# A planned attention-and-MLP kernel on one core: the second softmax's scores read in a burst, plans a batch deeper, batch 0's rows transposed on TensorE, output evictions chosen by stretch

## The chip, the core and the metric

The kernel runs on one core of a Trainium2 chip. A core has TensorE for matrix products (PE in the profile, PEld for its weight loads), VectorE (DVE), ScalarE (ACT), GpSimd (POOL) and SyncE (SP). They run at the same time, each through its own instruction queue in order, and wait for each other through semaphores. SyncE issues all DMA transfers of this kernel, between DRAM and the on-chip memory SBUF. PSUM holds TensorE's results and has eight banks of 128 partitions x 512 fp32. The metric is the device time of one execution in microseconds; lower is better.

## What is computed

```python
def mab(q, kv):                      # attention with kv as keys and values
    s = scale * (q @ kv.transpose(0, 2, 1))
    s = s - s.max(-1, keepdims=True)
    a = np.exp(s)
    a /= a.sum(-1, keepdims=True) + 1e-09
    return a @ kv
h = mab(I, x)                        # x: 4 x 12480 x 128, I: 32 inducing rows for each batch
y = mab(x, h).reshape(-1, 128)       # every row of x attends to the 32 rows of h
r = np.maximum(y @ w_in, 0.0)        # w_in: 128 x 2048
return (r * r) @ w_out               # w_out: 2048 x 128
```

There are two softmaxes. The first is over the 12480 rows of a batch, for each of 32 inducing rows, and gives `h`. The second is over the 32 rows of `h`, for each row of `x`. The MLP with a squared relu follows.

## The kernel before

Each of the four batches has 12480 rows. They are cut into 26 chunks of 480 rows, or into seven groups (six of four chunks, one of two); `WID` is a group's width in one of four quarters, 480 or 240 columns. x comes from DRAM in two layouts: `xT` (channels on partitions; the scores' moving operand, one load of 960 KB to a group into a tile `xp`) and `xn` (rows on partitions; the first softmax's values, in 13 halves of 448 or 512 KB into the five buffers `xnb`).

The kernel does not multiply by `w_in` row by row. Since y is a weighted mean of the 32 rows of h, the MLP's hidden values are linear in the 32 weights, and a batch's MLP is rewritten as a quadratic form of those weights. The work of a batch has four background parts, written as Python generators, and a foreground:

- `first(b)`, line 268: seven score steps (four products into one PSUM bank of the pool `ps_a`, then L298 on DVE, which scales them into `sT` and takes their maximum), then the overall maximum, exponentials on ACT (L323), 32x32 transposes on DVE (L333) and the weighted sum over `xn` on TensorE (`hacc`, L345). Each group's `hacc` is copied or added to `hq` on DVE (L351, L353). At its end stands `hT` (L365). The five first `xnb` loads are issued at score step 3, and each later one when a half has been used (`load_xn`, line 275).
- `prepare(b)`, line 457: products of `hT` with the weights, a long chain of small DVE instructions, products of columns on DVE (`G`, L518), and four weight products on TensorE (`wq`, L527) that give `st.w16`, the stationary operands of the foreground's last product.
- `second(b, G)`, line 368: scores of a group against `hT`, transposed on DVE into a tile `e2` of a pool of two (L381), maximum (L383), subtraction on POOL (L387), exponential on ACT (L388), sums and reciprocal on DVE (L391 to L393), product on POOL (L394), transpose back (L397), rounding to fp16 (L404 on ACT or L406 on DVE, and L407), and a store to a DRAM buffer `ad` (L408).
- `squares(b, G)`, line 433: loads `dT` from `ad` (L428), makes single squares (L442 into a bank of `ps_a`, L448, and L452 on POOL) and puts them into `dT` by DMA (L454).
- The foreground is the chunk. `up` (L638) multiplies `dT` by constant pairs into two double banks `hp`; `lift` (L647, twice to a chunk) squares them on ACT; `down` (L653, L654) multiplies by `w16` and `lin` into `po` (two banks of the pool `ps_o`); an eviction to `o` on ACT (L657) or DVE (L659), and the store (L660). Which engine evicts is decided while the program is written, by `to_act`, which keeps estimated totals for both.

The order: a prologue narrows the 64-bit weights on DVE (`narrow`, lines 236 to 242), runs `first(0)`, `prepare(0)` and the first two groups of `second(0, ...)`. Then 104 chunks run, and between them `background(k)` steps generators from a list `plan` by due times in chunk units. `spread(gen, steps, start, length)` enters `steps` steps from `start` on. `head` is the due time of `prepare(b)`, 26b the batch's first chunk. The program's instructions are then put in order at build time by a simulated timeline (`schedule_with_timeline_sim=True`): an instruction that is not ready there can be passed by later ones, so a due time sets a priority and not a place. SP's DMA issues are one such queue.

An `xp` tile (nine buffers, `NX`) is filled by `load_xT` (line 255), read by `first`'s scores and again by `second`'s; its buffer comes free for the next batch only then. So `second`'s reads, due at `reads[b, G]`, set when the next batch's loads can start.

A branch at the end, not taken here, recomputes everything in another way if a check on the data fails.

Of the kernel before, what the change touches and what calls it, by code (L numbers as in the profile page):

```python
# [17 lines left out]
P = 128  # L18
NB = 4
# [10 lines left out]
NQ = 4  # L30
MX = 16
# [15 lines left out]
def attend_then_relu2_mlp(ctx: ExitStack, tc: tile.TileContext, xn, xT, indT, w_in, w_out, outT):  # L47
# [168 lines left out]
    def load_words(src, name):  # L216
        wd = start.tile([P, 512, 2], U32, tag="words", name=name, bufs=6)
        nc.sync.dma_start(wd.rearrange("p (f d) w -> p f (d w)", d=P) if len(src.shape) == 3 else wd.rearrange("p n w -> p (n w)"), src)
        return wd

    def load_rows(j):
        wd = start.tile([P, 512, 2], U32, tag="words", name=f"wo{j}", bufs=6)
# [31 lines left out]

    def load_xT(b, G, again=False):
# [12 lines left out]
    def first(b):  # L268
# [6 lines left out]
        def load_xn(h):  # L275

            if h >= 2 * NG - 1:
                return None
            t = xnb[h % XB]
            rows = xn[b, 4 * CH * (h // 2):min(4 * CH * (h // 2 + 1), NT)]  # L280
            if h < 2 * NG - 2:
                k = 8 - h % 2
                nc.sync.dma_start(t[:, 0:k], rows.rearrange("(p t) c -> p t c", t=15)[:, 8 * (h % 2):8 * (h % 2) + k])
            else:
                nc.sync.dma_start(t[:, 0:7], rows[0:7 * P].rearrange("(p t) c -> p t c", t=7))
                for q in range(4):
                    nc.sync.dma_start(t[32 * q:32 * q + 16, 7], rows[7 * P + 16 * q:7 * P + 16 * q + 16])
            return t
# [14 lines left out]
        xns = xns or {h: load_xn(h) for h in range(XB)}  # L303
# [25 lines left out]
        hq = work.tile([P, P + 1], F32, tag="hq", name=f"hq_{b}", bufs=1)  # L329
        for G, nb32 in enumerate(BLK):  # L330
# [8 lines left out]
            hacc = side_psum(f"hacc_{b}_{G}")  # L339
            for t in range(nb32):  # L340
                if t % 8 == 0:
                    h = 2 * G + t // 8
                    xg = xns.pop(h)
                q = t % 4
                st.last = nc.tensor.matmul(  # L345
                    hacc[32 * q:32 * q + 32, 0:P], en[:, t], xg[:, t % 8], start=t < 4, stop=t + 4 >= nb32,
                )
                if t % 8 == 7 or t == nb32 - 1:
                    xns[h + XB] = load_xn(h + XB)
            if G == 0:  # L350
                nc.vector.tensor_copy(hq[:, 0:P], hacc[:, 0:P])  # L351
            else:
                nc.vector.tensor_tensor(hq[:, 0:P], hacc[:, 0:P], hq[:, 0:P], op=ALU.add)  # L353
            if G == NG - 1:
# [13 lines left out]
    def second(b, G, again=False):  # L368
# [10 lines left out]
        e = work.tile([P, 15, MI], F32, tag="e2", name=f"e2_{b}_{G}")  # L379
        ef = e.rearrange("p t i -> p (t i)")  # L380
        nc.vector.transpose(ef[:, 0:wb], ps[:, 0:wb])  # L381
        mx = work.tile([P, 15], F32, tag="mx2", name=f"mx2_{b}_{G}")
# [50 lines left out]
    def squares(b, G):  # L433
# [6 lines left out]
        ps = att_psum(f"sq_{b}_{G}")  # L440
# [187 lines left out]
    class Chunk:  # L628
# [14 lines left out]
        def lift(self, j):  # L643
# [3 lines left out]
            nc.scalar.activation(self.g[:, 2 * j:2 * j + 2], self.hp.pop(j)[:, 0:2, 0:CH], AF.Square)  # L647

        def down(self):
# [6 lines left out]
            if to_act(220 + 0.833 * CH, 110 + 1.042 * CH):  # L656
                nc.scalar.activation(o, po[:, 0:CH], AF.Identity, bias=st.bias, scale=st.osc)  # L657
# [16 lines left out]
    for G in range(NG):  # L674
        sts[0].xp[G] = load_xT(0, G)
# [34 lines left out]
    plan = []  # L710
# [9 lines left out]
    reads = {}  # L720
# [22 lines left out]
    spread(smallest(), 1, reads[NB - 1, NG - 1] + 3, 0)  # L743
# [11 lines left out]
    soon = chain(second(0, 0), second(0, 1))  # L755
# [11 lines left out]
    for n, chunk in enumerate(chunks):  # L767
        nxt = chunks[n + 1] if n + 1 < len(chunks) else None
        for j in (0, 1):
            chunk.lift(j)  # L770
            if nxt:
                nxt.up(j)
            if j == 0 and n:
                done = chunks[n - 1].down()
# [6 lines left out]
    chunks[-1].down()  # L781
# [192 lines left out]
```

## Time and profile before

| | us |
|---|---|
| median of 3 runs | 462.41 |
| lowest, highest run | 461.12, 466.04 |
| profiled execution | 464.73 |
| its span in the profile | 463.0 |
| first lift of the loop (start) | 87.10 |
| last lift of the loop (start) | 454.47 |

The profile records one execution. Engine lines give busy time, its share of the span and the number of instructions. Groups are named by source line, engine, operation, output and inputs by the program's names; behind the bar stand total busy time and the mean in ns, then the idle time of the engine just before them and what ended most of it. In a table by stage each row is a stretch of the span in us, its length, and busy us with the number of instructions for each engine, then the granted TensorE clock, the share of the DMA engines and GB/s. Rows of the timeline begin with start and duration in us; a bracket tells how long the engine was idle before and what released it.

### The profile page before, as it was taken

The page shows a single profiled execution, that of the slowest core. Times are in us where ns is not written, and L with a number is a line of the kernel's source. Part 1 is how long each engine was busy: PE and PEld are TensorE (multiplying, and loading weights), DVE is VectorE, ACT ScalarE, POOL GpSimd, SP SyncE. Part 2 cuts the span into 40 slices and gives each one's busy share as a digit, 9 for nine tenths or more (in the row PEclk, how much of TensorE's full clock was granted, in tenths as well). Part 3 has the DMA queues.
Part 4 walks back from the last instruction along what each step waited for, and adds up shares of the span by engine and source line. Part 5 has one row for each costly group of instructions (what it writes and reads, how often), then busy time and mean ns, then how long its engine had stood idle before and what let it go on. Part 6 is the DMA issues. An engine that isn't in the chain of part 4 may idle for free.

```text
span 463.0 us, 8566 instructions
## 1 busy us (share of the span) xinstructions
PE 366.8 (79%) x2979; PEld 163.2 (35%) x2979; DVE 325.7 (70%) x902; ACT 282.0 (61%) x397; POOL 85.9 (19%) x93
## 2 busy tenths in 40 slices
PE   0644744899979889878789888988879898788994
PEld 0003413543335333333244234433433344343441
DVE  8969378685643199497561899689626999996442
ACT  1004123479994497437567798566666878067993
POOL 1000011141210030232200132144100423340000
PEclk9999975699979799799599999999999999999998
DMA  7999980377759983667889958644794354337432
GB/s 296 421 248 392 372 295 24 97 240 249 207 173 337 335 277 101 197 188 187 266 276 293 344 195 244 195 138 145 240 290 154 102 167 165 101 128 231 151 136 105
DMA packets 64771, 100.71 MB, mean 218 GB/s; under 512 B 22992, under 2 KB 53968, under 8 KB 64720
## 3 DMA queue, kind: packets, MB, share of 16 engines
q1 hardware_dynamic: 64720, 100.09, 66.3%
q8 instruction: 25, 0.41, 0.4%
q14 instruction: 26, 0.21, 0.1%
HBM read 64.91 MB, written 31.95 MB: 209 GB/s over the span
## 4 chain that ended last, share of the span: by engine, by line
PE 30%; DVE 28%; DMA 26%; ACT 6%; issue 5%; SPq 2%; POOL 1%; ACTq 0%; DVEq 0%; POOLq 0%
DMA xnb<-xn_dram 8%; PE hp L638 8%; PE po L653 7%; ACT g L647 5%; DMA outT_dram<-o 5%; PE s L264 4%; PE hacc L345 4%; DMA xp_False<-xT_dram 4%; DMA dT<-zz 3%; DVE o L659 3%; DVE G L518 3%; DVE a L407 2%; PE wq L527 2%; DMA wo<-w_out_dram 2%; DMA dT<-ad 2%
## 5 line engine op out<-in xcount | busy, mean ns | idle before, releaser
L647 ACT ACTIVATE g<-hp 128x960 f16<-128x960 f32 x208 | 194.4, 974 | 60.7 <-PE hp L638 48.2
L638 PE MATMUL hp<-dT,pairs 96*128 96x480 f16 x416 | 121.4, 381 | 7.3 <-ACT g L647 4.9
L653 PE MATMUL po<-g,w 128*128 128x480 f16 x416 | 115.8, 377 | 7.6 <-ACT o L657 3.4
L387 POOL TENSOR_TENSOR e<-e,mx 128x480 f32<-128x480 f32 (+1 forms) x28 | 28.0, 999 | 232.2 <-DVE mx L383 76.3
L659 DVE TENSOR_SCALAR o<-po,osc,bias 128x480 f32<-128x480 f32 x60 | 45.4, 763 | 30.5 <-PE po L654 17.8
L653 PEld LDWEIGHTS <-w 128*128 128x128 f16 x416 | 40.6, 100 | 60.7 <-issue 19.3
L638 PEld LDWEIGHTS <-pairs 96*128 96x128 f16 x416 | 35.8, 101 | 66.6 <-issue 42.1
L345 PE MATMUL hacc<-xnb,en 128*32 128x128 f32 x784 | 38.3, 324 | 16.8 <-DMA xnb<-xn_dram 8.7
L264 PE MATMUL s<-xp_False,indT_sb 128*32 128x480 f32 (+1 forms) x224 | 32.9, 665 | 22.4 <-DMA xp_False<-xT_dram 12.1
L654 PE MATMUL po<-dT,lin 128*128 128x480 f16 x104 | 39.1, 379 | 7.7 <-DMA dT<-zz 7.5
L452 POOL TENSOR_TENSOR zz<-z 128x480 f16<-128x480 f32 (+1 forms) x28 | 30.2, 1078 | 66.3 <-DVE z L448 39.8
L323 ACT ACTIVATE sT<-sT,nb 128x480 f32<-128x480 f32 (+1 forms) x28 | 18.2, 658 | 33.5 <-DVE nb L316 33.5
L394 POOL TENSOR_TENSOR e<-e,z 128x480 f32<-128x480 f32 (+1 forms) x28 | 27.0, 967 | 56.1 <-DVE z L393 36.9
L345 PEld LDWEIGHTS hacc<-xnb,en 128*32 128x32 f32 x784 | 24.4, 126 | 33.6 <-DMA xnb<-xn_dram 9.7
L657 ACT ACTIVATE o<-po,bias,osc 128x480 f32<-128x480 f32 x44 | 33.0, 762 | 5.2 <-DMA outT_dram<-o 4.4
L353 DVE TENSOR_TENSOR hq<-hacc,hq 128x128 f32<-128x128 f32 x24 | 7.0, 291 | 37.6 <-PE hacc L345 37.6
L264 PE MATMUL s<-xp_False,hT 128*32 128x480 f32 (+1 forms) x224 | 27.7, 563 | 4.3 <-DVE k L195 1.4
L448 DVE TENSOR_SCALAR z<-sq,off,cut 128x480 f32<-128x480 f32 (+1 forms) x28 | 21.5, 767 | 9.3 <-PE sq L442 9.3
L518 DVE TENSOR_TENSOR G<-hwp,hw 128x512 f16<-128x512 f16 x64 | 24.9, 455 | 4.1 <-PE wq L527 4.1
L388 ACT ACTIVATE e<-e 128x480 f32<-128x480 f32 (+1 forms) x28 | 16.2, 578 | 17.0 <-POOL e L387 17.0
L404 ACT ACTIVATE a<-a,lessen 128x480 f16<-128x480 f32 (+1 forms) x20 | 13.6, 681 | 16.5 <-DVE a L397 16.3
L298 DVE TENSOR_SCALAR_CACHE_REDUCE sT<-s 128x480 f32<-128x480 f32 (+1 forms) x28 | 17.0, 608 | 9.1 <-PE s L264 9.1
(190 smaller groups left out, 419.2 us busy)
## 6 DMA issues: line engine op xcount, KB each, us to landing
outT_dram<-o SPq DMA_DIRECT2D x104, 240.0 KB, 2.8
xp_False<-xT_dram SPq DMA_DIRECT2D x24, 960.0 KB, 6.8
xnb<-xn_dram SPq DMA_DIRECT2D x28, 448.0 KB, 5.2
xnb<-xn_dram SPq DMA_DIRECT2D x24, 512.0 KB, 5.9
dT<-ad SPq DMA_DIRECT2D x72, 120.0 KB, 2.6
ad<-a SPq DMA_DIRECT2D x24, 240.0 KB, 2.5
dT<-zz SPq DMA_DIRECT2D x104, 30.0 KB, 2.3
wi<-w_in_dram SPq DMA_DIRECT2D x4, 512.0 KB, 5.6
```

The lines of the kernel that those rows point to most:

```text
L264: nc.tensor.matmul(ps[32 * q:32 * q + 32, 0:w], lhsT, xp[:, w * q:w * q + w], start=True, stop=True,)
L345: st.last = nc.tensor.matmul(hacc[32 * q:32 * q + 32, 0:P], en[:, t], xg[:, t % 8], start=t < 4, stop=t + 4 >= nb32,)
L387: nc.gpsimd.tensor_tensor(e[:, 0:t], e[:, 0:t], mx[:, 0:t].unsqueeze(2).broadcast_to([P, t, MI]), op=ALU.subtract)
L394: nc.gpsimd.tensor_tensor(e[:, 0:t], e[:, 0:t], z[:, 0:t].unsqueeze(2).broadcast_to([P, t, MI]), op=ALU.mult)
L452: nc.gpsimd.tensor_tensor(g[rows], zv[rows], zv[rows], op=ALU.mult)
L518: tt(g[:, :, MI * j:MI * j + n], hwp[:, :, 0:n], hw16f[:, :, s0:s0 + n], op=ALU.mult)
L638: nc.tensor.matmul(hp[:, i, 0:CH].rearrange("p (q t) -> p q t", q=4), pairs[0:96, (2 * j + i) * P:(2 * j + i + 1) * P], self.dT[0:96], sta ...
L647: nc.scalar.activation(self.g[:, 2 * j:2 * j + 2], self.hp.pop(j)[:, 0:2, 0:CH], AF.Square)
L653: nc.tensor.matmul(po[:, 0:CH], st.w16[:, i], self.g[:, i], start=i == 0, stop=False)
L654: done = [nc.tensor.matmul(po[:, 0:CH].rearrange("p (q t) -> p q t", q=4), st.lin, self.dT, start=False, stop=True)]
L657: nc.scalar.activation(o, po[:, 0:CH], AF.Identity, bias=st.bias, scale=st.osc)
L659: done.append(nc.vector.tensor_scalar(o, po[:, 0:CH], st.osc, st.bias, op0=ALU.mult, op1=ALU.add))
```

## The change

1. `second` keeps its transposed scores in a resident tile `scored` of eight slots and yields right after the transpose, so that a step of its own reads `xp`. In the plan that step is due at `reads[b, G]` (`READ`), and the other four at `rests[b, G]` (`REST`). The next batch's load of the group is due 0.4 chunk units after the read. `NX` is seven for nine. `head` of batch b may be as early as 26(b-1) + 0.6; before it was 26b - 17.
2. Batch 0's `xT` is not loaded. Its 13 halves of `xn` all have places of their own from the start (`homes`: the five `xnb`, four in `scored`, four in tiles that are used later), and `turn` transposes them on TensorE, 15 blocks of 128x128 to a group, into `hp` banks, from where ACT copies them to `xp`.
3. `hacc` is one PSUM bank over all seven groups, copied once; the adds to `hq` go.
4. The eviction of `po` goes to ACT in the stretches from a `head` to 18 chunks after it (`heavy`), and to DVE elsewhere; the last one goes to ACT.
5. The products of `squares` go into the `po` banks in place of `ps_a`'s; the 64-bit weight words have four buffers for six.

```diff
-NX = 9
+NX = 7
+HEAVY = 18
-MOST = 17
-PACE = (1.2, 2, 2, 3)
-EARLY = -1
+SLOTS = 8
+READ = (0, 2, 1, 1)
+REST = 2.6
...
+        def turn(G):
+            w = WID[G]
+            xp = st.xp[G] = flow.tile([P, 4 * CH], F32, tag="xp", name=f"xp_{b}_{G}", bufs=NX)[:, 0:4 * w]
+            to = xp.rearrange("p (q n) -> p q n", q=4)
+            for h in range(2 * G, min(2 * G + 2, HALVES)):
+                k = 8 - h % 2
+                ps = two_banks(f"xt_{h}").rearrange("p a (t c) -> p (a t) c", c=P)
+                for t in range(k):
+                    nc.tensor.transpose(ps[:, t], xns[h][:, t], ident)
+                whole = k if h < HALVES - 1 else 7
+                c0 = 256 * (h % 2)
+                nc.scalar.copy(
+                    to[:, :, c0:c0 + 32 * whole].rearrange("p q (t r) -> p t q r", r=32),
+                    ps[:, 0:whole].rearrange("p t (q r) -> p t q r", q=4),
+                )
...
-        xns = {}
+        xns = st.rows if not b else {}
         for G, w in enumerate(WID):
             if b and G == 3:
                 xns = {h: load_xn(h) for h in range(XB)}
+            if not b:
+                turn(G)
...
-            hacc = side_psum(f"hacc_{b}_{G}")
+            hacc = hacc or side_psum(f"hacc_{b}")
...
-            if G == 0:
+            if G == NG - 1:
                 nc.vector.tensor_copy(hq[:, 0:P], hacc[:, 0:P])
-            else:
-                nc.vector.tensor_tensor(hq[:, 0:P], hacc[:, 0:P], hq[:, 0:P], op=ALU.add)
...
-        e = work.tile([P, 15, MI], F32, tag="e2", name=f"e2_{b}_{G}")
+        if again:
+            e = work.tile([P, 15, MI], F32, tag="e2", name=f"e2_{b}_{G}")
+        else:
+            k = 480 * ((NG * b + G) % SLOTS)
+            e = scored[:, k:k + 480].rearrange("p (t i) -> p t i", i=MI)
         ef = e.rearrange("p t i -> p (t i)")
         nc.vector.transpose(ef[:, 0:wb], ps[:, 0:wb])
+        yield
...
-        ps = att_psum(f"sq_{b}_{G}")
+        ps = ps_o.tile([P, 512], F32, tag="po", name=f"sq_{b}_{G}")
...
-            if to_act(220 + 0.833 * CH, 110 + 1.042 * CH):
+            if act:
...
-    for G in range(NG):
-        sts[0].xp[G] = load_xT(0, G)
+    scored = flow.tile([P, SLOTS * 480], F32, tag="scored", name="scored", bufs=1)
+    homes = list(xnb)
...
+    sts[0].rows = {h: load_half(0, h, homes[h]) for h in range(HALVES)}
...
+    scored_by = {(b, G): second(b, G) for b in range(NB) for G in range(NG)}
     for b in range(NB):
-        head = -3.5
+        head = -4
         if b:
             sums = first(b)
             for G in range(NG):
-                free = max(0, G + NG - NX)
-                start = max(reads[b - 1, free] + 0.6, EARLY if b == 1 else -9)
+                start = reads[b - 1, G] + 0.4
                 spread(loads(b, G), 1, start, 0)
-                spread(sums, 1, start + 3, 0)
-            start += 3.5
+                start = max(start + 2.5, 26 * (b - 2) + 7 + 1.4 * G)
+                spread(sums, 1, start, 0)
+            start += 1
             spread(sums, 18, start, LONG)
-            head = max(start + LONG + LAG, 26 * b - MOST)
+            head = max(start + LONG + LAG, 26 * (b - 1) + 0.6)
             spread(prepare(b), 19, head, WEIGHTS)
+        busy.append((head, head + HEAVY))
         for G in range(NG):
-            reads[b, G] = head + 0.5 + PACE[b] * G
+            gen = scored_by[b, G]
+            reads[b, G] = head + 0.5 + (READ[b] if b else 0.4) * G
+            rest = rests[b, G] = max(reads[b, G] + 0.6, head + 1 + REST * G if b else 4 * G - 10)
             if b or G > 1:
-                spread(second(b, G), 4, reads[b, G], 2)
+                spread(gen, 1, reads[b, G], 0)
+                spread(gen, 4, rest, 2)
             if b or G > 0:
-                start = max(26 * b + 4 * G - 9, reads[b, G] + 2.1)
+                start = max(26 * b + 4 * G - 9, rest + 2.1)
...
-                done = chunks[n - 1].down()
+                done += chunks[n - 1].down(heavy(n - 1))
...
-    chunks[-1].down()
+    chunks[-1].down(True)
```

More of the change, by code (lines that the diff above doesn't have):

```diff
@@ L221, in load_rows @@
     def load_rows(j):
-        wd = start.tile([P, 512, 2], U32, tag="words", name=f"wo{j}", bufs=6)
+        wd = start.tile([P, 512, 2], U32, tag="words", name=f"wo{j}", bufs=4)
         for q in range(4):
@@ L252, in prepare_w_out, with load_half @@
         nc.scalar.mul(w_hi, wo_sb, t)
+    def load_half(b, h, t):
+        rows = xn[b, 4 * CH * (h // 2):min(4 * CH * (h // 2 + 1), NT)]
+        if h < HALVES - 1:
+            k = 8 - h % 2
+            nc.sync.dma_start(t[:, 0:k], rows.rearrange("(p t) c -> p t c", t=15)[:, 8 * (h % 2):8 * (h % 2) + k])
+        else:
+            nc.sync.dma_start(t[:, 0:7], rows[0:7 * P].rearrange("(p t) c -> p t c", t=7))
+            for q in range(4):
+                nc.sync.dma_start(t[32 * q:32 * q + 16, 7], rows[7 * P + 16 * q:7 * P + 16 * q + 16])
+        return t
     def load_xT(b, G, again=False):
@@ L275, in load_xn @@
         def load_xn(h):
[L277 to L281, printed above, removed]
-                k = 8 - h % 2
-                nc.sync.dma_start(t[:, 0:k], rows.rearrange("(p t) c -> p t c", t=15)[:, 8 * (h % 2):8 * (h % 2) + k])
-            else:
[L285 to L288, printed above, removed]
-        xns = {}
+            return load_half(b, h, xnb[h % XB]) if h < HALVES else None
+        def turn(G):
[3 more added lines that the diff above has]
+            for h in range(2 * G, min(2 * G + 2, HALVES)):
+                k = 8 - h % 2
+                ps = two_banks(f"xt_{h}").rearrange("p a (t c) -> p (a t) c", c=P)
[7 more added lines that the diff above has]
+                )
+                if whole < k:
+                    nc.scalar.copy(to[:, :, 224:240], ps[:, 7].rearrange("p (q r) -> p q r", q=4)[:, :, 0:16])
+        xns = st.rows if not b else {}
         for G, w in enumerate(WID):
@@ L301, in first @@
             yield
-        xns = xns or {h: load_xn(h) for h in range(XB)}
         m1 = small("m1")
@@ L329, in first @@
         hq = work.tile([P, P + 1], F32, tag="hq", name=f"hq_{b}", bufs=1)
+        hacc = None
         for G, nb32 in enumerate(BLK):
@@ L345, in first @@
                 st.last = nc.tensor.matmul(
-                    hacc[32 * q:32 * q + 32, 0:P], en[:, t], xg[:, t % 8], start=t < 4, stop=t + 4 >= nb32,
+                    hacc[32 * q:32 * q + 32, 0:P], en[:, t], xg[:, t % 8], start=G == 0 and t < 4, stop=G == NG - 1 and t + 4 >= nb32,
                 )
-                if t % 8 == 7 or t == nb32 - 1:
+                if b and (t % 8 == 7 or t == nb32 - 1):
                     xns[h + XB] = load_xn(h + XB)
-            if G == 0:
+            if G == NG - 1:
                 nc.vector.tensor_copy(hq[:, 0:P], hacc[:, 0:P])
-            else:
-                nc.vector.tensor_tensor(hq[:, 0:P], hacc[:, 0:P], hq[:, 0:P], op=ALU.add)
-            if G == NG - 1:
                 nc.vector.tensor_reduce(hq[:, P:P + 1], zs, axis=AX.X, op=ALU.add)
@@ L655, in down @@
             o = work.tile([P, CH], F32, tag="o", name=f"o_{self.b}_{self.c}", bufs=3)
-            if to_act(220 + 0.833 * CH, 110 + 1.042 * CH):
-                nc.scalar.activation(o, po[:, 0:CH], AF.Identity, bias=st.bias, scale=st.osc)
+            if act:
+                done.append(nc.scalar.activation(o, po[:, 0:CH], AF.Identity, bias=st.bias, scale=st.osc))
             else:
@@ L673, in attend_then_relu2_mlp @@
     w_words = [load_words(w_in[:, 1024 * j:1024 * j + 1024], f"wi{j}") for j in range(4)]
-    for G in range(NG):
-        sts[0].xp[G] = load_xT(0, G)
+    scored = flow.tile([P, SLOTS * 480], F32, tag="scored", name="scored", bufs=1)
+    homes = list(xnb)
+    for t0, t1 in ((0, 7), (7, 15), (15, 22), (22, 30)):
+        homes.append(scored[:, t0 * P:t1 * P].rearrange("p (t c) -> p t c", c=P))
+    homes += [flow.tile([P, 8, P], F32, tag="G", name=f"place{i}", bufs=2) for i in range(2)]
+    homes += [start.tile([P, 8, P], F32, tag="rows", name=f"rows{i}", bufs=2) for i in range(2)]
+    nc.vector.memset(homes[HALVES - 1][:, 7], 0.0)
+    sts[0].rows = {h: load_half(0, h, homes[h]) for h in range(HALVES)}
     def weights():
@@ L708, in smallest, with heavy @@
         yield
-    plan = []
+    plan, busy = [], []
+    def heavy(n):
+        return any(a <= n < z for a, z in busy)
     def spread(gen, steps, start, length):
@@ L718, in loads @@
         yield
-    reads = {}
+    reads, rests = {}, {}
+    scored_by = {(b, G): second(b, G) for b in range(NB) for G in range(NG)}
     for b in range(NB):
-        head = -3.5
+        head = -4
         if b:
@@ L753, in background @@
             due = next(todo, None)
-    soon = chain(second(0, 0), second(0, 1))
+    soon = chain(scored_by[0, 0], scored_by[0, 1])
     for n, _ in enumerate(prepare(0)):
@@ L769, in attend_then_relu2_mlp @@
         for j in (0, 1):
-            chunk.lift(j)
+            done = [chunk.lift(j)]
             if nxt:
```

10 lines of the change are left out of this document (6 added, 4 removed).

## The prediction, made before the changed kernel was built or run

> **What bounds the kernel now.** I read the page's busy shares first, then the busy time by stage, then the ACT lifts by stage as the clock of the loop, then the rows at the slow stages.
>
> ```profile
> PE 366.8 (79%) x2979; PEld 163.2 (35%) x2979; DVE 325.7 (70%) x902; ACT 282.0 (61%) x397; POOL 85.9 (19%) x93
> L647 ACT ACTIVATE g<-hp 128x960 f16<-128x960 f32 x208 | 194.4, 974 | 60.7 <-PE hp L638 48.2
> L659 DVE TENSOR_SCALAR o<-po,osc,bias 128x480 f32<-128x480 f32 x60 | 45.4, 763 | 30.5 <-PE po L654 17.8
> L657 ACT ACTIVATE o<-po,bias,osc 128x480 f32<-128x480 f32 x44 | 33.0, 762 | 5.2 <-DMA outT_dram<-o 4.4
> L353 DVE TENSOR_TENSOR hq<-hacc,hq 128x128 f32<-128x128 f32 x24 | 7.0, 291 | 37.6 <-PE hacc L345 37.6
> ```
>
> No engine is full over the span, so the answer lies in stages. Next, busy time by stage (columns: PE, PEld, DVE, ACT, POOL, granted clock, DMA share, GB/s); the last row is the whole loop.
>
> ```profile
> 0.00:60.00 60.00, 27.20 (x263) 10.74 (x267) 44.31 (x133) 7.95 (x17) 1.19 (x9) 1.00 0.98 347
> 60.00:87.00 27.00, 12.77 (x127) 7.68 (x120) 21.64 (x82) 7.47 (x12) 4.12 (x4) 0.58 0.44 145
> 87.00:136.00 49.00, 46.27 (x315) 18.12 (x313) 32.35 (x85) 43.83 (x68) 14.05 (x15) 0.95 0.64 204
> 136.00:163.00 27.00, 23.98 (x263) 12.26 (x263) 7.57 (x21) 15.09 (x20) 0.00 (x0) 0.81 0.92 309
> 256.00:325.00 69.00, 60.15 (x465) 25.60 (x463) 60.11 (x170) 51.89 (x77) 21.37 (x19) 1.00 0.65 205
> 355.00:390.00 35.00, 31.71 (x225) 14.00 (x226) 35.00 (x93) 29.43 (x39) 10.75 (x10) 1.00 0.37 119
> 390.00:410.00 20.00, 15.27 (x142) 7.94 (x141) 18.90 (x53) 5.92 (x9) 7.10 (x8) 0.91 0.41 125
> ...
> 87.00:459.00 372.00, 326.88 (x2595) 144.77 (x2593) 259.78 (x688) 266.56 (x368) 80.59 (x80) 0.95 0.64 204
> ```
>
> Before 60 us the DMA queues are full (0.98). In the loop DVE and ACT have nearly equal work, 259.78 and 266.56 us of 372, but at different times: 87 to 136 is ACT's, 136 to 163 is a transfer's (DVE 7.57 of 27), 355 to 410 is DVE's. The lifts alone (two to a chunk) show what that costs:
>
> ```profile
> 136.00:163.00 27.00, 11.52 (x13) 0.81 0.92 309
> 163.00:195.00 32.00, 14.38 (x16) 0.89 0.62 196
> 195.00:214.00 19.00, 4.02 (x5) 1.00 0.53 157
> 256.00:325.00 69.00, 33.77 (x36) 1.00 0.65 205
> 355.00:390.00 35.00, 25.37 (x28) 1.00 0.37 119
> 390.00:410.00 20.00, 4.29 (x5) 0.91 0.41 125
> 410.00:459.00 49.00, 40.61 (x44) 1.00 0.51 170
> ```
>
> Two stages nearly stop: 195 to 214 and 390 to 410, five lifts each. In both, the last weight product of a batch's `prepare` comes near the end, and only then do `po` and the lifts go on:
>
> ```profile
> 208.98 1.05 PE L527 MATMUL wq<-w_hi,G 128*128 128x128 f16 x16 [1.10 <-DVE wm L529]
> 210.91 0.38 PE L653 MATMUL po<-g,w 128*128 128x480 f16 x1
> ...
> 405.42 1.06 PE L527 MATMUL wq<-w_hi,G 128*128 128x128 f16 x16
> 407.64 0.38 PE L653 MATMUL po<-g,w 128*128 128x480 f16 x1 [0.80 <-DVE w L179]
> ```
>
> So the first chunks of batches 1 and 3 wait for a `prepare` that is late, while DVE (18.90 of 20) does it together with second's softmax and ACT (5.92) starves. After 410 nothing is left for the background and a lift costs 49/44 = 1.11 us.
>
> **The change, part by part.** Terms are against the profiled execution: 464.73 us, of which 463.0 are span; the median of the runs is 462.41, 2.3 below it, and I take that off at the end.
>
> *1. Plan a batch deeper.* By the plan's formulas prepare(b) begins at chunk 13.9, 35.0, 61.0 (b = 1, 2, 3) before, and at 10.8, 35.2, 53.6 after (for b = 3 after: second's last read of batch 2 at 35.2 + 0.5 + 6 = 41.7, its load 0.4 on, the score 2.5 on, then 1 + LONG + LAG = 9). Batch 1 gains 3 chunks, batch 2 nothing, batch 3 over 7. Three chunks at the pace of 256 to 325 (69/36 = 1.92 us a lift, 3.8 a chunk) are 11 us of lead, against a stall of 19 us less the five lifts' own 9.6: the stall of batch 1 goes, 9.4 us. Batch 3 has 28 us of lead against 20 us less 5 x 35/28 = 6.3: 13.7 us go. Bounds: 0 (the lead is eaten on the way) to 23.1; I take 23.1, as each lead is longer than its stall. Next late in their place are `dT` loads.
>
> *2. Second's scores in a burst.* Score matmuls and first transpose of each group are the same instructions, moved forward into eight resident slots; groups of batch 0 are then finished over 4G-10 in place of 1.2G-3 chunks. That moves work from 87 to 136, where ACT is nearly full (43.83 of 49), into 136 to 163. These rows price it and the reads:
>
> ```profile
> L381 DVE STREAM_TRANSPOSE e<-s 128x480 f32<-128x480 f32 x24 | 16.2, 674 | 3.5 <-PE s L264 3.3
> L388 ACT ACTIVATE e<-e 128x480 f32<-128x480 f32 (+1 forms) x28 | 16.2, 578 | 17.0 <-POOL e L387 17.0
> L404 ACT ACTIVATE a<-a,lessen 128x480 f16<-128x480 f32 (+1 forms) x20 | 13.6, 681 | 16.5 <-DVE a L397 16.3
> ```
>
> Five groups x (0.58 + 0.68) = 6.3 us of ACT. Bounds 0 and 6.3; I take 6.3, since the receiving stage has ACT free (15.09 of 27). Five more reads come before the first chunk (5 x 0.67 = 3.4 us); DVE's idle 5.4 us of 60 to 87 cover them, and without that cover they cost the 3.4.
>
> *3. Loads pulled forward.* With the rows of batch 0 read early, seven loads of batch 1 go out at once, ahead of `ad` and `dT` on the one SP queue, and the `xnb` loads right behind them. The last of seven such loads at the start took this long to land:
>
> ```profile
> xp_False<-xT_dram SPq DMA_DIRECT2D x1, 480.0 KB, 17.8
> 81.71 2.59 SPq L428 DMA_DIRECT2D dT<-ad  x5
> ```
>
> A `dT` of the prologue queued behind them waits 0 to 15 us. DMA is busy 0.44 in 60 to 87, so most should have landed; I take +3.
>
> *4. Evictions by stretch.* Heavy stretches hold 65 chunks (18 each, the first 29 joined) and the last goes to ACT too: 66 on ACT for 44, so 22 x 0.76 = 16.6 us leave DVE and 22 x 0.75 = 16.5 join ACT. Where it tells, 355 to 390, DVE is at 35.00 and ACT at 29.43; the stage's evictions on DVE are
>
> ```profile
> 355.00:390.00 35.00, 8.80 (x12) 1.00 0.37 119
> ```
>
> and with them ACT would need 38, more than 35: alone this gains nothing there. Level, both need 32.2. Bounds +3 and -5; I take -3 with the earlier prepare.
>
> *5. hacc kept in PSUM, squares' matmul in `po`'s buffers.* 21 adds of 0.29 us leave the loop's DVE (6.1 us). On the path the hacc stage waits for `xnb`, so 0 (bounds 0 to -6). A `po` buffer held until DVE's `z` can stop `down`: 0 to 0.76 a group, a pass like L659's. Taken as 0 together.
>
> *6. Startup.* 6.4 MB of xT loads go (some 18 us of a full queue at 347 GB/s). New: 98 transposes, 14 PSUM copies on ACT (idle there, 7.95 of 60, 1 us each by the lift). The old rows:
>
> ```profile
> 12.11 1.83 PE L264 MATMUL s<-xp_False,indT_sb 128*32 128x480 f32 x8 [12.11 <-DMA xp_False<-xT_dram]
> 29.94 1.03 PE L264 MATMUL s<-xp_False,indT_sb 128*32 128x240 f32 x8 [1.76 <-DVE sT L298]
> 37.41 1.93 PE L345 MATMUL hacc<-xnb,en 128*32 128x128 f32 x30 [2.11 <-DVE en L333]
> 54.15 2.02 PE L345 MATMUL hacc<-xnb,en 128*32 128x128 f32 x30 [0.40 <-DVE hq L353]
> 59.37 0.19 DVE L365 TENSOR_TENSOR hT<-hs,zr 128x32 f32<-128x32 f32 x1
> 97.77 1.01 PE L264 MATMUL s<-xp_False,hT 128*32 128x480 f32 x8
> 99.53 0.49 PE L617 MATMUL cm<-ident,cm 128*1 128x128 f32 x3
> 211.73 0.27 PE L617 MATMUL cm<-ident,cm 128*1 128x128 f32 x1
> 75.00 0.50 PEld L546 LDWEIGHTS pl<-inc,before 128*128 128x128 f32 x2 [2.53 <-issue]
> ```
>
> A score group takes 1.83 us here and 1.01 later: TensorE runs at half rate (the clock column's 1.00 before its first record says nothing). A transpose follows the last at (0.49 - 0.27)/2 = 0.11 us at full rate, so 0.22 at half; its weight load is 0.25. At half rate: 98 x 0.22 to 0.25 + 6.5 x 1.83 = 33 to 36 us from about 10.7 (a half load has half the bytes of the xT load that let PE start at 12.11, 1.4 us less at 347 GB/s), so 44 to 47; then the old 6.4 us from scores to hacc (30.97 to 37.41), hacc without DVE's 0.40 gaps 6.5 x 2.05 = 13.3, or 10.4 if the rate doubles midway, and 1.9 to `hT`: 63 to 69 against 59.6, +3 to +9. At full rate PE is out of the way; DVE's own 44.31 us, less 2 of adds, with some waits left (an estimate) put `hT` near 49: -10. I take +4: the densest row of this stage, 2.02 at 54.15, is still at half rate.
>
> The Trainium skill, "TensorE: Matmul & The Clock Gate", Part 4 (PE-mode transpose), says that transposes do not count as a busy PE and leave the clock low. It speaks against this part; by it the startup stays at +4 and the sum at 437, without it it may be -10 and the sum 423. No run here yet shows a stretch of transposes.
>
> Sum: 464.7 - 23.1 - 6.3 - 3 + 3 + 4 = 439.3; less 2.3, **437**. Cross-check: the loop's ACT becomes 283, DVE 237; in a loop of 372 - 29 = 343 their mean share is 0.76, against 0.71 now and 0.81 in 256 to 325.
>
> **Rivals.**
> *B, the clock rises.* PE works without gaps from 11 us, the rate doubles, startup is -10 for +4: 423. Against it, the half-rate rows above.
> *C, ACT takes DVE's place.* Up to chunk 72 ACT carries 65 evictions (49), 144 lifts at 194.4/208 (135) and its other 266.6 - 194.4 - 33.0 = 39: 223 us, at the 0.895 it reached in 87 to 136 (43.83 of 49) 249. Three hacc stages in which it waits 12 (27.00 - 15.09) add 36. With 87 + 4 before, 64 lifts x 1.11 = 71 after and 4 to the end that is 451 of span, 450 on the median's scale.
> *E, the order does not follow the plan.* prepare(1) was planned from 13.9 and ran its last product at 209 us, chunk 28: the schedule set by simulated readiness can keep stalls. Then only -9.3 and +7 remain: 460.
> *D, slower: the queue.* Each burst of xT and xnb loads stands before `dT` and output writes on the one queue. At 15 us each for two bursts, with startup at +9: 437 + 30 + 5 = 472. It decides from about 15 us a burst on; against it, loads in batches 2 and 3 are still 1 to 2 chunks apart.
>
> **How the numbers follow.** The likeliest case 0.46 (own range 425 to 449); B 0.16; C 0.17; E 0.09; D 0.12. The range 412 to 462 takes in A, B, C and E and leaves D out, with 5 us below B for a loop that gains its bounds. Under 1% either way can hardly be told from no change: faster by over 1% (below 457.8) is A + B + C = 0.79, within 1% is E = 0.09, slower D = 0.12.
>
> **What would show it.** Right: lifts never under eight in 20 us after 100 us; the last `wq` of batch 3 well before chunk 78; some 30 chunks at 1.1 us a lift at the end; score groups of 1.8 us in a startup whose `hT` comes at 62 to 68. Wrong: `hT` near 49 (B); ACT above 90% through two heavy stretches (C); a five-lift stage at `wq` again (E); `dT` landing in over 12 us with PE behind it (D).

## The result and the profile after

| kernel | median us (lowest to highest, runs) | ratio to before, 95% interval |
|---|---|---|
| before | 461.76 (461.07 to 466.04, 4) | 1 |
| after | 440.61 (438.60 to 442.46, 4) | 0.9522 [0.9445, 0.96] |

The change makes the kernel 4.8% faster, 21 us. The ratios are worked out without the slowest executions, so they are not exactly the quotients of the medians. The profiled execution of after took 438.60 us, of which 436.8 are span. Predicted were 437 us. The experiments below show that the number came out right although its steps did not: the part that brings the gain had been taken as 0, and the part that was to bring it costs time.

First the page of after: its line of busy shares, and the groups of lifts and evictions.

```profile
PE 361.5 (83%) x3077; PEld 171.4 (39%) x3077; DVE 310.4 (71%) x846; ACT 313.5 (72%) x444; POOL 89.4 (20%) x93
L673 ACT ACTIVATE g<-hp 128x960 f16<-128x960 f32 x208 | 193.7, 971 | 33.0 <-PE hp L664 31.1
L683 ACT ACTIVATE o<-po,bias,osc 128x480 f32<-128x480 f32 x66 | 49.9, 758 | 9.2 <-issue 4.1
L685 DVE TENSOR_SCALAR o<-po,osc,bias 128x480 f32<-128x480 f32 x38 | 29.5, 776 | 35.2 <-PE po L680 27.3
```

ACT has taken 22 evictions, as counted ahead, and the lifts' idle time fell from 60.7 to 33.0 us. The lifts by stage, the clock of the loop:

```profile
92.00:106.00 14.00, 1.66 (x2) 1.00 0.24 65
106.00:126.00 20.00, 7.47 (x8) 0.83 0.60 210
194.00:213.00 19.00, 9.20 (x10) 1.00 0.70 220
357.00:377.00 20.00, 10.96 (x12) 0.91 0.46 146
380.00:433.00 53.00, 47.41 (x52) 1.00 0.53 168
```

The two stages with five lifts are gone. The last `wq` of batch 1 ends at 194.1 us here and that of batch 3 at 377.2; ten lifts stand in the 19 us ahead of the first and ten behind it (194 to 213), and twelve ahead of the second (357 to 377). One new stall stands at 92 to 106, with two lifts. At the end 52 lifts run at 53/52 = 1.02 us. Where the end of the batches' chain moved is read from the four `hT` writes (first and last start), in before,

```profile
L365 DVE TENSOR_TENSOR hT<-hs,zr x4: 191/191/192, 59.4 to 349.2; 128x32 f32<-128x32 f32 x4
```

and in after, here with the last weight products of batches 0 and 3:

```profile
L386 DVE TENSOR_TENSOR hT<-hs,zr x4: 184/192/192, 52.9 to 317.6; 128x32 f32<-128x32 f32 x4
...
104.22 1.06 PE L553 MATMUL wq<-w_hi,G 128*128 128x128 f16 x16
...
376.10 1.07 PE L553 MATMUL wq<-w_hi,G 128*128 128x128 f16 x16
```

The last `hT` is at 317.6 us for 349.2 before, 31.6 earlier; the last `wq` at 376.1 for 405.4, 29.3 earlier. The span is shorter by 26.2: by these marks it is gained ahead of the last `hT`, and some 5 us are lost again behind it.

### The profile page after: what moved, and what is told of

Same layout as the page of the kernel before. It is cut to its first block, busy times and chain, and to the rows that moved or that the text cites. A ratio compares the mean times of both kernels' runs of the same rounds, so it can differ in the third digit from the quotient of the medians.

```text
span 436.8 us, 8776 instructions
## 1 busy us (share of the span) xinstructions
PE 361.5 (83%) x3077; PEld 171.4 (39%) x3077; DVE 310.4 (71%) x846; ACT 313.5 (72%) x444; POOL 89.4 (20%) x93
## 5 line engine op out<-in xcount | busy, mean ns | idle before, releaser
L683 ACT ACTIVATE o<-po,bias,osc 128x480 f32<-128x480 f32 x66 | 49.9, 758 | 9.2 <-issue 4.1
L413 POOL TENSOR_TENSOR scored<-scored,mx 128x480 f32<-128x480 f32 (+1 forms) x28 | 28.9, 1033 | 125.9 <-DVE k L198 56.8
L685 DVE TENSOR_SCALAR o<-po,osc,bias 128x480 f32<-128x480 f32 x38 | 29.5, 776 | 35.2 <-PE po L680 27.3
L357 DVE STREAM_TRANSPOSE en<-sT 128x480 f32<-128x480 f32 (+1 forms) x28 | 17.9, 642 | 28.7 <-PE hacc L369 23.7
L369 PE MATMUL hacc<-xnb,en 128*32 128x128 f32 x664 | 28.3, 296 | 11.2 <-DMA xnb<-xn_dram 6.6
L420 POOL TENSOR_TENSOR scored<-scored,z 128x480 f32<-128x480 f32 (+1 forms) x28 | 27.7, 994 | 36.7 <-DVE z L419 20.9
L369 PEld LDWEIGHTS hacc<-xnb,en 128*32 128x32 f32 x664 | 19.4, 116 | 23.1 <-DMA xnb<-xn_dram 9.0
L430 ACT ACTIVATE a<-a,lessen 128x480 f16<-128x480 f32 (+1 forms) x28 | 18.6, 666 | 12.3 <-DVE a L423 3.1
L305 ACT COPY xp<-xt 128x896 f32<-128x896 f32 (+1 forms) x13 | 12.3, 956 | 17.6 <-PE xt L302 17.6
L278 PE MATMUL s<-xp_False,indT_sb 128*32 128x480 f32 (+1 forms) x168 | 21.0, 569 | 4.6 <-DMA xp_False<-xT_dram 3.2
L278 PE MATMUL s<-xp_False,hT 128*32 128x480 f32 (+1 forms) x168 | 20.4, 553 | 3.3 <-DVE z L418 1.9
```

Of the source, the lines that this page charges most:

```text
L278: nc.tensor.matmul(ps[32 * q:32 * q + 32, 0:w], lhsT, xp[:, w * q:w * q + w], start=True, stop=True,)
L369: st.last = nc.tensor.matmul(hacc[32 * q:32 * q + 32, 0:P], en[:, t], xg[:, t % 8], start=G == 0 and t < 4, stop=G == NG - 1 and t + 4 >= ...
L413: nc.gpsimd.tensor_tensor(e[:, 0:t], e[:, 0:t], mx[:, 0:t].unsqueeze(2).broadcast_to([P, t, MI]), op=ALU.subtract)
L420: nc.gpsimd.tensor_tensor(e[:, 0:t], e[:, 0:t], z[:, 0:t].unsqueeze(2).broadcast_to([P, t, MI]), op=ALU.mult)
L683: done.append(nc.scalar.activation(o, po[:, 0:CH], AF.Identity, bias=st.bias, scale=st.osc))
L685: done.append(nc.vector.tensor_scalar(o, po[:, 0:CH], st.osc, st.bias, op0=ALU.mult, op1=ALU.add))
```

## The experiments

Each kernel undoes or adds one piece, of after unless said otherwise. Chips differ, so ratios are to the kernel before as it ran on the same chip. Groups are counted from 0, so group 3 is the fourth.

| edit | median us | ratio [95%] |
|---|---|---|
| squares' products back in `ps_a` | 457.36 | 0.9936 [0.9891, 0.9981] |
| **before** with squares' products in `po` banks | 440.28 | 0.9552 [0.9421, 0.9682] |
| **plan of before**, all else of after | 430.86 | 0.9328 [0.9272, 0.9383] |
| evictions by totals again | 446.39 | 0.9682 [0.9607, 0.9758] |
| xT of batch 0 loaded, ahead of the rows | 454.90 | 0.9882 [0.9811, 0.9952] |
| the same, rows written behind `w_out` | 444.57 | 0.964 [0.9545, 0.9735] |
| `hacc` per group, with adds | 442.43 | 0.9596 [0.9513, 0.9679] |
| two rotating tiles for eight slots | 439.98 | 0.9575 [0.9467, 0.9682] |
| prepare(3) due at 61 again | 441.19 | 0.9574 [0.9499, 0.9649] |
| second(0) behind prepare(0) | 446.00 | 0.9677 [0.9589, 0.9765] |
| second behind the next `en`, from group 3 | 446.07 | 0.9705 [0.9581, 0.9829] |
| the same, from group 4 | 434.43 | 0.9469 [0.9335, 0.9602] |

**1. The squares' bank, undone.**

```diff
-        ps = ps_o.tile([P, 512], F32, tag="po", name=f"sq_{b}_{G}")
+        ps = att_psum(f"sq_{b}_{G}")
```

> The changed kernel with squares' products in the one bank of ps_a again, shared with both kinds of scores. Prediction: 0 in either direction (438 to 444 us). Rival: the bank is held for squares while reads and sums of the hT chain want it, 28 times up to 1 us: 445 to 455 us.

457.36 us, above the rival's range too: 17 us of the 21 are gone with this one line. What the bank does shows first in TensorE's timeline behind the first `hT`. With the shared bank:

```profile
64.67 1.93 PE L560 MATMUL R<-wo_sb,hwS 128*32 128x128 f32 x32 [4.89 <-DVE hwS L529]
...
79.23 0.59 PE L468 MATMUL sq<-dT,singles 96*32 96x480 f16 x4
...
83.31 1.01 PE L278 MATMUL s<-xp,hT 128*32 128x480 f32 x8
```

and in after:

```profile
60.84 1.83 PE L278 MATMUL s<-xp,hT 128*32 128x480 f32 x8 [0.93 <-DVE inv_t L197]
```

The program writes squares(0, 0) ahead of the third group of second. With one bank for both, the third group's scores came at 83.31 and not at 60.84; the second group's had come at 57.8 and 57.6. The bank went first to `sq`, at 79.23, which needs prepare's `singles` and a `dT` that passes through two transfers, issued here at

```profile
72.76 1.67 SPq L434 DMA_DIRECT2D ad<-a  x2
75.29 2.71 SPq L454 DMA_DIRECT2D dT<-ad  x6
```

TensorE itself was idle in between (4.89 us at one place). So the single bank works as a queue in the order in which the program is written, and whoever waits at its head for a transfer or another chain holds up scores that are ready. No row names this as a long wait, as the instructions behind stand late in their engine's own order; that the ordering at build time put them there is inferred.

But this first place shows the order and not the loss. With the shared bank prepare(0) even ends 13 us earlier (last `wq` at 92.2 for 105.3), and chunk 50 is lifted first at 271.6 us for 284.2. The time goes behind that. The lifts there, with the shared bank:

```profile
270.00:290.00 20.00, 5.16 (x7) 0.83 0.81 236
295.00:315.00 20.00, 5.08 (x6) 0.74 0.38 118
```

and in after:

```profile
270.00:290.00 20.00, 11.16 (x12) 1.00 0.73 241
295.00:315.00 20.00, 9.34 (x10) 1.00 0.81 281
```

From chunk 50 to chunk 56 pass 42 us for 22. `hT` of batch 2 is 12 us late (244.1 for 232.3), and the squares are later still: those of batch 1's last group come at 297.5 for 265.3 and those of batch 2's first at 301.5 for 272.4, in turn with the scores of batch 3 (at 295.3 and 299.6) in the one bank. The chunks' last product reads these squares in `dT`. So by these traces the shared bank delays both the scores that lead to `hT` and the squares that the chunks need.

**2. The squares' bank alone, in the kernel before.** Same line, other direction, nothing else changed.

> The kernel before, with one edit: the squares' products of prepare are accumulated in one of the banks that the output products use, in place of the bank that scores, sums and reads share. All else is as before. Theory 1 (the shared bank is the main part by itself: putting the squares back cost the changed kernel 17 us): 442 to 452 us, ratio 0.96 to 0.98, with each hT at least 3 us earlier than before and the stall at 195 to 214 shorter. Rival (the bank tells only with the deeper plan and the loads read early, since before, each hT waits for its rows anyway): 458 to 465, ratio 0.99 to 1.005. Third, slower: a bank of the output products held until DVE's z delays the down products, up to 0.76 us a group over 24 groups: 465 to 480.

440.28 us, 22.4 below before on that chip and as fast as the whole change, a little better than theory 1. First the lifts in the two stages that end with the last `wq` of batches 1 and 3 (at 201.5 and 382.4 us here); the like stages had five lifts each before:

```profile
182.00:201.00 19.00, 9.79 (x12) 1.00 0.86 257
...
362.00:382.00 20.00, 10.65 (x12) 0.97 0.34 106
```

Both stalls are gone with the plan of before. Then who waited for the bank's `sq` tiles, in before:

```profile
who waited for it (us, times):
  POOL zz L452: 39.8, 12
  DVE z L448: 9.3, 8
  PEld s L264: 5.2, 5
  PE s L264: 3.3, 2
  PEld mb L314: 1.7, 2
```

With the squares in `po`, the waits of scores (`s`) and of the maximum (`mb`) leave this list; 0.8 us of an eviction and 0.4 of a `down` come in, so the feared price of a held `po` bank is small:

```profile
who waited for it (us, times):
  POOL zz L452: 51.7, 15
  DVE z L448: 3.7, 4
  DVE o L659: 0.8, 1
  PEld hacc L345: 0.4, 1
  PE po L653: 0.4, 1
```

The waits that left are 5.2, 3.3 and 1.7 us, 10.2 at most, and don't make 22. More than half must come in another way; that it is the order in which the instructions stand is likely, but not shown. What moves are the scores of the next batch's first softmax (`indT_sb`), here batch 2's last group behind a square of batch 1, in before:

```profile
211.93 0.39 PE L442 MATMUL sq<-dT,singles 96*32 96x480 f16 x4
213.76 0.61 PE L264 MATMUL s<-xp_False,indT_sb 128*32 128x240 f32 x8
```

and with the squares in `po`, where the next square comes later:

```profile
193.38 0.61 PE L264 MATMUL s<-xp_False,indT_sb 128*32 128x240 f32 x8 [0.46 <-DVE e L381]
...
205.14 0.39 PE L442 MATMUL sq<-dT,singles 96*32 96x480 f16 x4
```

The last score group (240 columns), on which `hT` of batch 2 depends, moves from 213.76 to 193.38. The first two squares of batch 1 stand ahead of it in both kernels; the whole series runs earlier and closer, its seven groups starting within 36 us (from 157.33) for 44 (from 169.87). It adds up over the batches (first and last `hT`):

```profile
L365 DVE TENSOR_TENSOR hT<-hs,zr x4: 191/191/192, 59.6 to 327.0; 128x32 f32<-128x32 f32 x4
```

From 59.4 and 349.2 before to 59.6 and 327.0: nothing at the start and 22.2 us at the last batch, of the 25.3 between the two profiled spans (463.0 and 437.7). The shares of waits at run time and of the order fixed at build time were not separated; that would need the one's order with the other's bank, and it was not tried.

**3. The plan of before in the changed kernel.** Heads, due times, `NX` of nine, no burst and `e2` tiles as before; startup by transposes, one `hacc` bank, evictions by `heavy` and squares in `po` stay. Since `heavy` follows the heads, its stretches move back too (69 evictions on ACT for 66).

```diff
-NX = 7
+NX = 9
...
-        head = -4
+        head = -3.5
...
-                start = reads[b - 1, G] + 0.4
+                free = max(0, G + NG - NX)
+                start = max(reads[b - 1, free] + 0.6, EARLY if b == 1 else -9)
...
-            head = max(start + LONG + LAG, 26 * (b - 1) + 0.6)
+            head = max(start + LONG + LAG, 26 * b - MOST)
...
-            reads[b, G] = head + 0.5 + (READ[b] if b else 0.4) * G
+            reads[b, G] = head + 0.5 + PACE[b] * G
```

> The changed kernel with the plan of before: heads, due times and pace of before, nine buffers of xT, second's scores read when their group is worked on (no burst, two rotating tiles), loads as before. Startup by transposes, hacc in one bank, squares in the output products' banks and evictions by stretch (over the heads of before) stay. The prediction's steps 1 to 3 put this part at 26.4 us: 460 to 468. Theory now (with the squares out of the shared bank the plan is worth nothing or costs, since the kernel before with the squares' bank alone is as fast as the changed one): the parts that stay are then worth their 4 to 6 us each on top of that run's 440.3: 428 to 437. Rival (the parts are not additive, they all buy the same time; ACT's 283 us and the startup set the rest): 438 to 445.

430.86 us, within the theory's range and the fastest of all; its interval lies clear of after's. The deeper plan, the burst and the early loads, with the stretches that follow them, together cost 0.9522/0.9328, 2.1% or some 10 us, where 26.4 of gain had been summed. By stages of this kernel: chunks 4 to 8 (107 to 123 us), and from the last `hT` to the last `wq` (321 to 369):

```profile
107.00:123.00 16.00, 13.09 (x136) 6.50 (x132) 10.16 (x26) 16.00 (x32) 3.64 (x4) 1.00 0.64 206
...
321.00:369.00 48.00, 43.83 (x363) 20.71 (x362) 42.51 (x123) 44.25 (x64) 17.28 (x17) 1.00 0.43 134
```

The same two in after (107 to 130 and 318 to 377; columns as in the tables by stage before):

```profile
107.00:130.00 23.00, 19.90 (x207) 9.35 (x206) 8.00 (x20) 17.50 (x31) 1.97 (x2) 0.85 0.70 241
...
318.00:377.00 59.00, 50.08 (x388) 22.93 (x387) 52.11 (x138) 49.50 (x70) 21.65 (x18) 0.97 0.41 130
```

From the first lift of chunk 4 to that of chunk 8 pass 21 us in after (109.2 to 130.1) and 16 here (107.0 to 122.8), where ACT is full. In after the hacc stage of batch 1 has been pulled into them (from 112.5 us; here from 117.5), and DVE does 8.00 of 23. Behind the last `hT`, prepare(3) needs 59 us in after and 48 here: 52.11 us of DVE for 42.51. Of the 9.6 us more, second's own instructions make 4.1 (27.1 for 23.0) and four evictions 3.1, where here there are none. `hT` of batch 1 came earlier by the deeper plan (138.6 us for 144.6), but the work moved out of its way came back in worse places. Which of the plan's pieces costs what was not split further, but for two: see 6.

**4. Evictions by the old totals.**

```diff
-            if act:
+            if to_act(220 + 0.833 * CH, 110 + 1.042 * CH):
```

> The changed kernel with the old rule for output evictions (estimated totals of both engines). Theory of the prediction: moving evictions from VectorE to ScalarE in the heavy stretches gains little by itself, up to 3 us: 440 to 444 us. Rival: in batch 3's prepare, where VectorE is busy 37.06 of 39 us, some 15 evictions of 0.76 us come back and make the stretch 8 to 12 us longer: 449 to 453 us.

446.39 us, 6 slower, between the theory's range and the rival's. 53 evictions are on DVE here for 38, and `hT` of batch 3 comes at 324.2 us for 317.6. The stage 357 to 380, in which prepare(3) runs, first here:

```profile
357.00:380.00 23.00, 17.61 (x145) 8.88 (x144) 22.72 (x62) 16.91 (x23) 8.02 (x9) 1.00 0.43 135
```

then in after:

```profile
357.00:380.00 23.00, 21.02 (x157) 11.73 (x157) 17.03 (x43) 16.74 (x24) 8.14 (x5) 0.93 0.49 154
```

With the old rule DVE is full there, 22.72 of 23; by stretches it is busy for 17.03, and the last `wq` ends 13 us earlier (377.2 for 390.5), of which 7 stand already at `hT`.

**5. Startup.** xT of batch 0 loaded again and no `turn`; in the second kernel the reads of the rows are also written behind those of `w_out`'s words.

```diff
-            if not b:
-                turn(G)
...
+    for G in range(NG):
+        sts[0].xp[G] = load_xT(0, G)
```

and in the second kernel also

```diff
-    sts[0].rows = {h: load_half(0, h, homes[h]) for h in range(HALVES)}
+    sts[0].rows = {}
...
+        sts[0].rows.update({h: load_half(0, h, homes[h]) for h in range(HALVES)})
```

> The changed kernel, but batch 0's xT is loaded again (6.4 MB ahead of its rows) and nothing is transposed on TensorE; all else as changed. Theory: the transposes brought hT from 59.6 to 53.1 us because TensorE's clock rose while they ran; without them hT is back at 59 to 61 us and the time at 445 to 449 us, 4 to 8 above the changed kernel's 440.6. Rival: between hT and the first chunks VectorE is the bound and swallows the difference: hT late, but the time within 2 us of 440.6.

> As the run without transposes, but the rows of batch 0 are traced behind w_out's words, so that half of those words go out among the rows (12 MB ahead of the last of them in place of 15). Theory: what the saved 6.4 MB buy is w_out narrowed on VectorE before hT, and not hT itself; with the words earlier, prepare(0) ends some 5 to 10 us before the 121 us of that run and the time is 446 to 451 us. Rival: the 14 us of that run come from TensorE's clock and the transposes themselves, whatever the order: 453 to 457 us.

454.90 and 444.57 us. In the first, theory and rival both fail: `hT` came at 48.2, before after's 52.9, although no transposes ran and each full score group took 1.83 us, and still 14 us were lost: the words of `w_out` stood behind twice 6.4 MB of loads, and their narrowing fell into prepare(0)'s time, where DVE then had no free microsecond:

```profile
48.00:92.00 44.00, 17.48 (x80) 3.23 (x80) 43.93 (x106) 10.94 (x18) 12.08 (x11) 0.54 0.74 249
```

In the second kernel the words go out among the rows, the first at 23.98 us for 37.04. Loading in place of transposing then costs 4 us, which the intervals don't tell from nothing. The order of the transfers on the one queue is worth 10 us, the two kernels' difference, more than the 6.4 MB saved.

**6. Pieces that made no measurable difference.** `hacc` per group with its adds; two rotating `e2` tiles in place of the eight slots (`if True:` for `if again:`); and prepare(3) due at 61, as before (`26 * (b - 1) + 0.6 if b < 3 else 61`).

> The changed kernel with one PSUM tile to a group for hacc and the six adds to hq on VectorE again. Prediction: the stage waits for xnb, so 0 to 6 us: near 441 us (438 to 444). Rival: the adds stand on the chain of the four hT, each group's products waiting for the add before (0.4 us and 0.3 us, six times): 2 to 4 us to a batch and 447 to 455 us.

> The changed kernel, but second's transposed scores go into two rotating tiles again in place of eight resident slots; the plan and its due times stay. Theory: every run so far ends 114 to 120 us after hT(3), so the loop is set by the chain from hT(b) over second's reads, the loads and first's sums to hT(b+1); two tiles hold the reads back, each hT comes 5 to 12 us later than the one before, and the time is 452 to 465 us. Rival: as with prepare(3)'s due time, the place of the reads matters little: 438 to 444 us.

> The changed kernel with one due time put back: prepare(3) may begin at chunk 61 at the earliest, as before, in place of 53.6; batch 3's second moves with it. Theory: the stall at chunk 80 was a late prepare(3); it comes back with some 10 to 15 us between chunks 78 and 82, and the time is 450 to 456 us. Rival: the loop is bound by what VectorE and ScalarE have to do in all, so the place of prepare(3) matters little: 438 to 443 us.

442.43, 439.98 and 441.19 us, all with intervals that overlap after's. The last tests the larger half of the prediction's main step, batch 3's: seven chunks of due time changed nothing, and the last `wq` ended at 379.2 us for 377.2. The lifts counted up to `hT` say why. `hT` of batch 3 comes at chunk 60.5 in both kernels, so a prepare that may begin at 53.6 has nothing to begin with; before, it came at 65.5 for a due time of 61.0.

The first kernel shows something else. With the adds, `hT` of batch 0 comes at

```profile
L389 DVE TENSOR_TENSOR hT<-hs,zr x4: 191/192/193, 58.4 to 324.7; 128x32 f32<-128x32 f32 x4
```

58.4 us for after's 52.9 and before's 59.4, although it transposes as after does and its score groups take 1.01 us too. So 5.5 of the 6.5 us by which the first `hT` came earlier are the one `hacc` bank's, and 1 is left to the transposes. The first lift is 6.5 us later (91.43 for 84.98); the medians differ by 1.8, which the intervals don't tell from nothing.

**7. The new stall at 92 to 106.** The maximum of second(0, G) from the third group on is held by an order edge behind prepare(0)'s last reduction (`gate`).

```diff
+        with tc.issue_after(sts[0].gate.ins) if b == 0 and G > 1 and not again else nullcontext():
+            nc.vector.tensor_reduce(mx[:, 0:t], e[:, 0:t], axis=AX.X, op=ALU.max)
```

> The changed kernel, but the maximum of second(0, G), G from 2 on, may not be issued on VectorE ahead of prepare(0)'s last reduction (an order edge, no new wait). Theory: the 14 us without lifts from 92 to 106 come from second's work of batch 0 that VectorE does between prepare(0)'s instructions; held back, the last wq of prepare(0) comes 8 to 14 us earlier and the time is 428 to 436 us. Rival: the work is only moved and the loop up to chunk 72 is full, so it costs the same later: 438 to 443 us.

446.00 us, 5 above after, with intervals that just meet. The last `wq` of prepare(0) came 5 us earlier (100.2 for 105.3), but `hT` of batch 1 came 7 later (145.8 for 138.6): the groups only moved into the next part of the chain. The stall is no dearer a place for them. It isn't the deeper plan's either: with the plan of before 13.2 us pass between two lifts from 90.3 on, and in before with the squares' bank alone 11.4 from 97.5 on, while with the shared bank the longest pause there is 5.9. It comes with the freed bank, which lets second's groups pass ahead of prepare(0) (see 1).

**8. Second's work moved into the hacc stages.** Its maximum for batches 0 to 2 is held behind the first transpose of the next batch's `en`, from group 3 or group 4 on; the later steps are due from there.

```diff
+        gate = sts[b + 1].entry if b + 1 < NB and G >= 3 and not again else None
+        with tc.issue_after(gate.ins) if gate else nullcontext():
+            nc.vector.tensor_reduce(mx[:, 0:t], e[:, 0:t], axis=AX.X, op=ALU.max)
```

> The changed kernel, with second's reduce of the groups from the fourth on, for batches 0 to 2, held by an order edge behind the first transpose of the next batch's first softmax, and their later steps due from there. It takes DVE work from the stretch in which prepare(b) and the sums of batch b+1 run, into the hacc stage, where DVE is busy 8.8 of 29, 16.6 of 35 and 8.4 of 27 us. Theory (prepare and the sums wait for DVE behind second's groups; hT comes earlier by what is moved, 4 groups of about 2 us): hT of batches 1 to 3 each 3 to 8 us earlier, wqend(0) near 99, 425 to 436 us. Rival (the work is only moved, and second's late finish delays prepare of the batch after, as gating it behind prepare's last reduce did): 438 to 448 us, with hT no earlier than 138, 232 and 317.

> As the run from the fourth group on, but from the fifth on: one group less for each batch is moved into the hacc stage. Theory: three quarters of that run's gain or, if its last groups are late for the next prepare, more: 427 to 437 us. Rival (only moved): 437 to 446 us.

446.07 and 434.43 us. From group 3 on, `hT` came 11, 13 and 7 us earlier, for batches 1 and 2 more than the theory gave, and the kernel was still no faster (its interval overlaps after's): the chunks of batch 0 that need these groups stood still (nine lifts in 33 us; ACT, granted clock, DMA):

```profile
118.00:151.00 33.00, 7.46 (x9) 0.74 0.84 281
```

With one group less to move, the gain in `hT` (6, 9 and 8 us) is kept. Its 434.43 is 6 us below after, but the intervals overlap, so that much is not shown.

## Why the prediction was right in its number and not in its steps

Three kernels make a chain from before to after, each with its own runs of before: 462.7 to 440.3 us by the squares' bank alone, to 430.9 by startup, `hacc` and evictions, and back up to 440.6 by the plan.

- **Step 1, the deeper plan (-23.1), failed.** The rows were read rightly as far as they go: both stalls stood where prepare of batches 1 and 3 was late, and they went. But the leads were counted in due times, and prepare waits for `hT`. Before, `hT` of batches 1 to 3 came at chunks 19, 39 and 65.5 (by the lifts), four to five behind the due times 13.9, 35.0 and 61.0. The prediction itself quoted against the step, under rival E, that prepare(1) was planned from chunk 13.9 and ended at chunk 28. What held `hT` back was in large part the bank: it came 22.2 us earlier for batch 3 with the bank alone, and a due time seven chunks later changed nothing. With the shared bank all the rest of the change brings that `hT` as early (328.0 us), and the time is 457.36 all the same: the lead is then eaten by the late squares (see 1).
- **Steps 2 and 3, burst and early loads (-6.3, +3), failed too.** Measured with step 1 they cost some 10 us in place of 26.4 of gain. Second's ACT time in 87 to 136 did fall, from 6.2 us to 1.4, but most of it went ahead of the loop and only 2.7 us stand in 136 to 163, where it had been expected. ACT, the reason for the move, is busy for only 29.84 us of the first 49 of the loop in after (85 to 134). In prepare(3) the later steps of second cost DVE time (see 3).
- **Step 4, evictions (-3)**: right in direction and place, undersized. Undone it costs 6 us, a little beyond the bound of -5, where -3 was taken.
- **Step 5 failed: `hacc` and the bank, taken as 0 together.** `hacc` at 0 holds for the time, though not for where it acts (see 6); 18 adds leave the loop (5.2 us), not 21 (6.1 us), as six of the 24 stand in the startup. For the bank only a cost was priced, a `po` buffer held too long (measured: 0.8 and 0.4 us of waits). Its other side, that the old bank comes free, was left out; that is the term of 17 to 22 us. No row that the prediction quotes names it, and the waits on `sq` in experiment 2, 5.2 and 3.3 us, look small. The Trainium skill, "Perfetto Trace Analysis", Optimizing Tensor Performance, Matmuls, has the rule: independent matmul groups should rotate through different PSUM banks. The experiments agree, with 22 us.
- **Step 6, startup (+4)**: wrong sign. The clock rose, as in rival B: score groups of 1.01 us, and `hT` at 52.9, near its 49 and not at 62 to 68. The rise kept the transposes from costing what was forecast, but the 6.5 us that `hT` gained are `hacc`'s for the most part (5.5, see 6). Of them only 2.1 reached the first lift (84.98 for 87.10): prepare(0) had to share DVE with more of second's groups, as the stage from `hT` on shows, with DVE 30.60 of 32.

```profile
53.00:85.00 32.00, 19.37 (x147) 7.16 (x148) 30.60 (x93) 10.82 (x18) 10.46 (x10) 0.57 0.67 222
```

- Of what was to show the steps right, "lifts never under eight in 20 us" held but for the stretch from 92 to 130 and seven in 158 to 178; the last `wq` "well before chunk 78" came 3 us before it (377.2 for 380); the end ran at 1.02 us a lift for 1.1.

So -23.1 - 6.3 - 3 + 3 + 4 and the measured -22.4 - 9.4 + 9.7 give -25.4 and -22.1, nearly the same sum by different terms. That the total came out is luck, and no evidence for its terms.

## What to carry to other kernels

Before planning work earlier, look at what a shared buffer of one makes of the plan: list its users in the order in which the program writes them, and ask of each what it waits for. One that waits for a transfer at the head of such a buffer delays all the others, and here that showed as late starts and idle engines, hardly as a wait. Ask also what a step really waits for before giving it an earlier due time. Test each part of a change alone and undone: here the best kernel (430.9 us, 2.0% below after) is the change without the part that gave it its name.

## What the hardware showed that was not expected

The granted clock rose in a stretch in which TensorE did nothing but transposes. The timeline of after at the start, and its stretches of one clock (PE, PEld, DVE, ACT, POOL, clock, DMA, GB/s):

```profile
11.31 5.14 PE L302 MATMUL xt<-ident,xnb 128*128 128x128 f32 x23 [11.31 <-DMA xnb<-xn_dram]
16.38 1.10 PE L278 MATMUL s<-xp,indT_sb 128*32 128x480 f32 x8
17.41 1.86 PE L302 MATMUL xt<-ident,xnb 128*128 128x128 f32 x15
```

```profile
13.20:16.60 3.40, 3.40 (x20) 3.04 (x22) 2.88 (x5) 2.03 (x3) 0.00 (x0) 1.00 1.03 408
...
33.70:37.10 3.40, 0.27 (x1) 0.08 (x1) 3.40 (x12) 0.00 (x0) 0.00 (x0) 1.00 0.59 185
37.10:43.90 6.80, 4.15 (x65) 3.42 (x65) 6.73 (x16) 4.66 (x14) 0.00 (x0) 0.50 0.20 61
```

Until 16.4 us a transpose takes 5.14/23 = 0.22 us, from then on 1.86/15 = 0.12, and the first score group takes 1.10 us for 1.83 before. The records of the clock begin at 16.61 us, with full rate (the column's 1.00 ahead of that says nothing); in the 3.4 us before, PE was busy 3.40 of 3.40, with transposes alone but for the last 0.2 us. In the kernel with the adds (experiment 6) the first record, full rate, is at 14.55 us and the first score product at 15.71, so there transposes alone came before it. After a stretch with 0.27 us of work it fell to 0.50. The Trainium skill, "TensorE: Matmul & The Clock Gate", Part 4 (PE-mode transpose), says that transposes do not count as a busy PE; the prediction weighed it at this place, and these two traces contradict it for this kernel's fp32 blocks of 128x128.
